# Gathering attention scores with one DMA per head, rows 13 partitions apart

## The chip, the cores and the metric

The kernel runs on one core of one Trainium2 chip. The metric is the device time of one execution in microseconds; a profiled execution also leaves a trace, from which the rows below are read. The engines are named as in the profile: PE (matmuls; PEld is its weight loads), DVE, ACT, POOL and SP, whose queue issues nearly all DMAs here.

## The reference

Attention with a mix over heads before and after the softmax, followed by a gated expert layer. Batch 4, 12 heads, 448 positions, head dimension 64; the layer has 1,792 tokens, width 768 and inner width 1,536. All in float32.

```python
def _attn_ref(q, k, v, w_pre, w_post):
    scores = (1 / sqrt(64)) * matmul(q, k.transpose(0, 1, 3, 2))
    scores = einsum('bhij,hg->bgij', scores, w_pre)       # pre-mix over heads
    scores = scores - max(scores, axis=-1, keepdims=True)
    attn = exp(scores)
    attn = attn / (sum(attn, axis=-1, keepdims=True) + 1e-09)
    attn = einsum('bhij,hg->bgij', attn, w_post)          # post-mix over heads
    return matmul(attn, v)

def _moe_ref(x, w_gate, w_val, w_out, rms_g):
    xn = x / sqrt(mean(x * x, axis=-1, keepdims=True) + 1e-06) * rms_g
    g = xn @ w_gate
    return (g * (1 / (1 + exp(-g))) * (xn @ w_val)) @ w_out
```

## The kernel before, in words

**Chunks, slots, pairs.** Each of the four batches is cut into four chunks of query rows, 16 chunks in all (`n`). A chunk of 120 rows has 24 slots of `RH` = 5 query rows each: 12 slots in each half `u` of the 128 partitions. Two slots of a half are one pair step `p`; the chunks have 6, 6, 6 and 5 pairs (`PAIRS`), so there are 92 steps. The last chunk of a batch has ten slots in its first half and eight in the second.

**Scores, gather, pre-mix.** `qk_mm` computes the scores of two heads into two PSUM tiles, query rows on the partitions and 448 keys along them. `qk_evac` copies each to a staging tile `st` in SBUF (eight buffers; ACT takes the even head, DVE the odd one). The pre-mix needs, for one slot, the five rows of all 12 heads side by side on the partitions. That regrouping is a DMA from SBUF to SBUF, the *gather*: for each head and each half, SP issues one DMA that writes five partitions of the target `r`, 12 apart, with up to 12 slots in each, 448 float32 (1,792 bytes) a slot.

```python
for u in range(2):
    slots = 2 * (np_ - (u == 1 and halves_of(n, np_ - 1) == 1))
    rows = slice(64 * u + h, 64 * u + h + H * (RH - 1) + 1, H)
    nc.sync.dma_start(rt[n][rows, :slots], st[64 * u : 64 * u + RH * slots])
```

A chunk thus has 24 gathers. `r` is a rotating tile with two buffers, a new one for each chunk, so chunk `n` is gathered while chunk `n - 1` is consumed. `premix` multiplies the 60 rows of a half (`HR` = 12 x 5) with `wk_pre`, in which the pre-mix weights are spread over a mask, slot by slot.

**The order of the work.** The schedule is written out by hand, in program order for each engine. In step `t`, PE does the pre-mix of step `t`, the post-mix of step `t - 1`, a share of the attention-times-value products (`av_mm`) of an earlier chunk, and a share of the scores of the next chunk. DVE takes the row maxima, ACT the exponentials with their sums, POOL scales the post-mix weights. The scores of chunk `n` are spread over the steps of chunk `n - 1`, ending two steps before the chunk starts; their copies and gathers follow one step later. Loads (`q`, `k`, `v`), the stores of the attention output to DRAM (`xd`), its reading back as `sq` for the norm, and an early conversion of part of the expert weights (`wraw`, `wac`) are jobs at fixed steps. All of them go through SP's queue, in order. Before step 0 stands a prologue: loads, all scores of chunk 0, its gathers, the first pre-mix.

**After the steps.** The expert layer follows: products with weights and tokens split into two parts, three matmuls for each. From the third token tile on, its tiles take the two buffers of `r` over (`x_tile`).

`layout` prepares the inputs on the host: it orders the query rows of a chunk so that a half's rows stand as row-in-slot times slots, starting at partition 0 and 64, and it repeats the pre-mix weights and the mask to fit the rows of `r`.

Of the kernel before, what the change touches and what calls it, by code (L numbers as in the profile page):

```python
# [7 lines left out]
F32 = mybir.dt.float32  # L8
F32R = mybir.dt.float32r
# [7 lines left out]
B, H, S, D = 4, 12, 448, 64  # L17
DM, DFF = 768, 1536
RH = 5
CHUNK = 120  # L20
NC = 4
PAIRS = [6, 6, 6, 5]
OFF = [0, 120, 240, 360]
SP_ = 460
HR = H * RH
JT = 64
JC, JP = 4, 112
KT, FT = DM // 128, DFF // 128
# [5 lines left out]
def attention_moe(ctx: ExitStack, tc, q, k, v, wpre, wpost, mask, ident, wgv, wo, rms_g, out):  # L34
    nc = tc.nc
    NCHUNK = B * NC

    def pool(stack, name, bufs=1, **kw):
        return stack.enter_context(tc.tile_pool(name=name, bufs=bufs, reuse_waits="tile", **kw))
# [17 lines left out]
    pr = pool(ctx, "pr", 2)  # L57
# [10 lines left out]
    wk_pre = cst.tile([128, 64], F32, name="wk_pre")  # L68
    wk = cst.tile([128, HR], F32, name="wk")

# [4 lines left out]
    def load_consts():  # L75
        nc.sync.dma_start(msk.rearrange("p a r -> p (a r)"), mask)
        nc.sync.dma_start(we, wpre)
        nc.sync.dma_start(wp, wpost)

    def setup():  # L80
        nc.vector.tensor_scalar(we, we, D ** -0.5, None, ALU.mult)
        nc.vector.memset(wk_pre, 0.0)
        for i, (o, w) in enumerate(((wk_pre[:, :HR], we), (wk, wp))):
            m = msk[:, i].unsqueeze(1).to_broadcast([128, H, RH])
# [3 lines left out]
    kt, qt, vt, rt, sps, et, sm, wn, at, pm, nmx, qps, xps, xt = ({} for _ in range(14))  # L88
# [18 lines left out]
    def halves_of(n, p):  # L107
        return 1 if n % NC == NC - 1 and p == PAIRS[-1] - 1 else 2

    def qk_mm(n, hp):  # L110
        ps = [ps_q.tile([128, 512], F32, name="qk", tag="qk") for _ in range(2)]
        for u in range(2):
            for j in range(2):
                sl, m = slice(64 * j, 64 * j + 64), slice(64 * u, 64 * u + 64)
                nc.tensor.matmul(ps[j][m, :S], qt[n][sl, hp, m], kt[n // NC, hp][sl], start=True, stop=True)  # L115
        qps[n, hp] = ps

    def qk_evac(n, hp, j):
        h, np_ = 2 * hp + j, PAIRS[n % NC]
        ps = qps[n, hp][j]  # L120
        st = pq.tile([128, S], F32, name="st", tag="st", bufs=8)
        if j:
            nc.vector.tensor_copy(st, ps[:, :S])  # L123
        else:
            nc.scalar.activation(st, ps[:, :S], AF.Copy)  # L125
        if h == 0:
            rt[n] = pr.tile([128, 2 * KT, S], F32, name=f"r{n}", tag="r")
        for u in range(2):
            slots = 2 * (np_ - (u == 1 and halves_of(n, np_ - 1) == 1))
            rows = slice(64 * u + h, 64 * u + h + H * (RH - 1) + 1, H)  # L130
            nc.sync.dma_start(rt[n][rows, :slots], st[64 * u : 64 * u + RH * slots])

    def premix(n, p):
        ps = [ps_s.tile([128, 512], F32, name="sp", tag="sp") for _ in range(halves_of(n, p))]
        for v_ in range(2):
            for u in range(len(ps)):
                sl = slice(64 * u, 64 * u + HR)
                o = ps[u][64 * v_ : 64 * v_ + 64, :S]
                nc.tensor.matmul(o, wk_pre[sl], rt[n][sl, 2 * p + v_], start=True, stop=True)  # L139
        sps[n, p] = ps  # L140
# [14 lines left out]
    def norm(n, p):  # L155
# [5 lines left out]
        nc.vector.reciprocal(r, t)  # L161
        wn[n, p] = pe.tile([128, 2, HR], F32, name="wn", tag="wn")
        for u in range(k_):
            nc.gpsimd.tensor_scalar(wn[n, p][:, u], wk, r[:, u : u + 1], 1.0, ALU.mult, ALU.mult)  # L164

    def postmix(n, p):
        ps = [ps_m.tile([128, 512], F32, name="pm", tag="pm") for _ in range(2)]
        e, w = et.pop((n, p)), wn.pop((n, p))
        for u in range(2):
            u_ = min(u, len(e) - 1)  # L170
            for c in range(JC):
                for m in range(2):
                    j = min(2 * c + m, S // JT - 1) * JT
                    for v_ in range(2):
                        sl = slice(64 * v_, 64 * v_ + HR)
                        at_ = (u * JC + c) * HR
                        o = ps[v_][64 * m : 64 * m + JT, at_ : at_ + HR]
                        nc.tensor.matmul(o, e[u_][sl, j : j + JT], w[sl, u_], start=True, stop=True)  # L178
        pm[n, p] = ps
# [15 lines left out]
    def av_mm(n, hp):  # L195
# [5 lines left out]
        for c_ in range(JC):  # L201
            for m in range(2 if c_ < JC - 1 else 1):
                sl = slice(64 * m, 64 * m + JT)
                for j in range(2):
# [98 lines left out]
    for n in range(NCHUNK):  # L303
        lo, hi = first[n + 1] + 1, first[n + 2] + 1
        for hp in range(H // 2):
            t = lo + hp * (hi - lo) // (H // 2)
# [7 lines left out]
    for n in range(NCHUNK):  # L314
        b, c = divmod(n, NC)
# [18 lines left out]
    def part_a(extra):  # L334
        for j in range(H // 4):
            load_q(0, j)
            load_k(0, j)
        load_consts()
        nc.vector.memset(ones, 1.0)
        for hp in range(H // 2):  # L340
            qk_mm(0, hp)
            for j in range(2):
                qk_evac(0, hp, j)
            if hp == 5:
                setup()
        load_q(1)
        nc.sync.dma_start(g_sb, rms_g)
        nc.sync.dma_start(eye, ident)
        done = []
        for t in range(T + 24):  # L350
            def back(lag):
                return steps[t - lag] if 0 <= t - lag < T else None

            if t == first[NCHUNK - 1]:
                qk_ctx.close()
                start_b()
            for f, *a in jobs_at[t]:
                f(*a)
            for a in done:
                x_store(*a)  # L360
            done = [(n, hp // 3) for n, hp in (av_at[t - 1] if t else []) if hp % 3 == 2]
            if back(0):
                premix(*back(0))
            for a in qk_at[t - 1] if t else []:
                for j in range(2):
                    qk_evac(*a, j)
            for a in done:
                av_copy(*a)
                av_sum(*a)
            if back(1):  # L370
                postmix(*back(1))
            for a in av_at[t]:
                av_mm(*a)
            for a in qk_at[t]:
                qk_mm(*a)
            if back(0):
                rowmax(*back(0))
                expo(*back(0))
            if back(1):
                for v_ in range(2):  # L380
                    evac_a(*back(1), v_)
            if back(0):
                norm(*back(0))
            extra(t - T)
            if t >= T + 6 and not done and not any(av_at[t:]):
                break
# [46 lines left out]
    def x_tile(i):  # L433
        if i < 2:
            t = b_pools["x"].tile([128, 2 * KT, S], F32R, name=f"x{i}", tag=f"x{i}")
        else:
            t = pr.tile([128, 2 * KT, S], F32R, name=f"x{i}", tag="r")
        return t[:, :KT], t[:, KT:]

    raws = {}  # L440
# [55 lines left out]
    w, xs, wos, hs, hr = {}, {}, {}, {}, []  # L496
# [219 lines left out]
def layout(inputs):  # L716

    import numpy as np

    q, k, v = inputs["q"], inputs["k"], inputs["v"]  # L720
    def pairs(x):
        return x.reshape(B, H // 2, 2, S, D).transpose(0, 2, 4, 1, 3).reshape(B, 2 * D, H // 2, S)

    qt = np.zeros((B, 2 * D, H // 2, SP_), np.float32)
    qt[..., :S] = pairs(q)
    ql = np.zeros((B, 2 * D, NC, H // 2, 2, 64), np.float32)
    for c, p in enumerate(PAIRS):
        for u in range(2):
            ns = 2 * (p - (u == 1 and c == NC - 1))
            r, s = np.meshgrid(np.arange(RH), np.arange(ns), indexing="ij")  # L730
            i = OFF[c] + u * 2 * RH * p + s * RH + r
            ql[:, :, c, :, u, : RH * ns] = qt[..., i.reshape(-1)]
    kl = pairs(k)
    vl = np.zeros((B, H, JC * 128, D), np.float32)
    vl[:, :, :S] = v
    vl = vl.reshape(B, H, JC, 128, D).transpose(0, 3, 1, 2, 4)

    def cols(w, kt):
        w = np.ascontiguousarray(w)
        if w.dtype != np.float64:  # L740
            raise TypeError(w.dtype)
        w = w.view(np.int64)
        return w.reshape(kt, 128, -1, 128).transpose(2, 1, 0, 3).reshape(-1, 128, kt, 128)

    def halves(x):
        return np.tile(np.pad(x, ((0, 64 - HR), (0, 0))), (2, 1))

    eye_r = np.eye(RH, dtype=np.float32)
    return {
        "q": ql.reshape(B, 2 * D, NC, H // 2, 128),  # L750
        "k": kl,
        "v": vl,
        "wpre": halves(np.tile(inputs["w_pre"], (RH, 1))),
        "wpost": halves(np.repeat(inputs["w_post"], RH, axis=0)),
        "mask": halves(np.concatenate([np.repeat(eye_r, H, axis=0), np.tile(eye_r, (H, 1))], axis=1)),
        "ident": np.eye(JP, dtype=np.float32),
        "wgv": np.concatenate([cols(inputs["moe_w_gate"], KT), cols(inputs["moe_w_val"], KT)], axis=2),
        "wo": cols(inputs["moe_w_out"], FT),
        "rms_g": inputs["moe_rms_g"].reshape(KT, 128).T,
    }  # L760
# [18 lines left out]
```

## Time and profile before

| | us |
|---|---|
| median of 3 runs (1039.56 to 1043.53) | 1042.5 |
| the profiled execution, own time | 1044.07 |
| its span | 1042.3 |
| PE busy in the span | 924.9 |
| DVE busy | 573.1 |
| ACT busy | 351.5 |
| POOL busy | 279.8 |

The mean granted clock of PE is 0.957 of full speed. Busy times overlap; PE's share of 89% is a mean over a stage that is nearly always busy and one that is not. Of the chain of work that ended last, PE holds 53%, DMA 19% (the gather `r<-st` alone 10%) and DVE 12%.

### The profile page before, as it was taken

Reading aid. Unit: us, or ns where it says so; the run is one execution under the profiler, and the core shown is the slowest. Engines: PE = TensorE matmul, PEld = TensorE weight load, DVE = VectorE, ACT = ScalarE, POOL = GpSimd, SP = SyncE. Lnnn points to the kernel's source line nnn. Section 1 sums busy time; section 2 is a strip of 40 time slices with the busy share of each in tenths; the row PEclk is TensorE's granted clock in tenths of the full one; section 3 lists DMA queues with packets and bytes.
Section 4 is the critical chain, followed back from the end, with each engine's and each line's share of the span. In section 5 each row is a group of like instructions: output and inputs, shape, how many; then the busy total and the mean of one; then the engine's idle time right before and its main releaser. Section 6 shows DMA issues by size and latency. Waiting matters only on the chain.

```text
span 1042.3 us, 29796 instructions
## 1 busy us (share of the span) xinstructions
PE 924.9 (89%) x12696; PEld 749.2 (72%) x12696; DVE 573.1 (55%) x990; ACT 351.5 (34%) x798; POOL 279.8 (27%) x349
## 2 busy tenths in 40 slices
PE   4669978887688688798989999999999999999998
PEld 0346655565356556565779999999999987999997
DVE  1447745764475466464495454555699977611100
ACT  1346635554554455566311101111111122421200
POOL 0011101111311221333445344444455562100000
PEclk9989989998898899898989999999999999999999
DMA  4535456545545545544422222122433346523100
GB/s 140 163 129 169 131 160 178 167 135 168 162 147 161 151 147 165 152 125 137 151 65 96 97 96 84 50 77 97 146 120 125 108 131 208 196 98 98 53 27 36
DMA packets 73108, 131.49 MB, mean 126 GB/s; under 512 B 19376, under 2 KB 63120, under 8 KB 72976
## 3 DMA queue, kind: packets, MB, share of 16 engines
q1 hardware_dynamic: 72688, 128.01, 38.5%
q8 instruction: 100, 1.64, 0.7%
q0 software_dynamic: 288, 1.57, 0.4%
q14 instruction: 32, 0.26, 0.1%
HBM read 67.90 MB, written 22.95 MB: 87 GB/s over the span
## 4 chain that ended last, share of the span: by engine, by line
PE 53%; DMA 19%; DVE 12%; ACT 5%; issue 4%; POOL 1%; SPq 1%; DVEq 0%; ACTq 0%; POOLq 0%
DMA r<-st 10%; PE po L493 6%; PE po L494 6%; PE po L492 6%; PE sp L139 4%; PE qk L115 4%; PE pm L178 4%; PE av L206 4%; PE pv L494 4%; PE pv L492 3%; PE pv L493 3%; DMA wraw<-in_wgv 3%; PE pg L492 3%; PE pg L494 3%; PE pg L493 3%
## 5 line engine op out<-in xcount | busy, mean ns | idle before, releaser
L152 ACT ACTIVATE e<-sp,nm 128x448 f32<-128x448 f32 x180 | 112.4, 629 | 166.0 <-DVE nm L145 166.0
L139 PE MATMUL sp<-r,wk_pre 60*64 60x448 f32 x720 | 124.3, 586 | 45.8 <-DMA r<-st 31.7
L178 PEld LDWEIGHTS pm<-wn,e 60*64 60x64 f32 x5888 | 115.8, 140 | 57.4 <-POOL wn L164 42.3
L164 POOL TENSOR_SCALAR wn<-wk,rp 128x60 f32<-128x60 f32 x180 | 55.1, 320 | 365.8 <-DVE rp L161 267.4
L115 PE MATMUL qk<-k,q 64*64 64x448 f32 x768 | 119.0, 602 | 23.6 <-ACT st L125 14.0
L145 DVE TENSOR_REDUCE nm<-sp 128x1 f32<-128x448 f32 x180 | 103.6, 616 | 55.5 <-PE sp L139 53.6
L206 PE MATMUL av<-a,v 64*64 64x120 f32 (+1 forms) x2688 | 107.1, 274 | 26.9 <-ACT xt L221 18.7
L178 PE MATMUL pm<-wn,e 60*64 60x60 f32 x5888 | 122.6, 226 | 6.4 <-issue 2.9
L139 PEld LDWEIGHTS sp<-r,wk_pre 60*64 60x64 f32 x720 | 45.1, 141 | 95.1 <-issue 47.5
L206 PEld LDWEIGHTS av<-a,v 64*64 64x64 f32 x2688 | 87.1, 141 | 32.4 <-ACT xt L221 19.8
L492 PE MATMUL pv<-x,wh 128*128 128x448 f32 x264 | 97.8, 371 | 2.3 <-ACT wh L424 2.3
L494 PE MATMUL pv<-x,wl 128*128 128x448 f32 x264 | 97.9, 371 | 1.2 <-POOL wl L425 1.2
L493 PE MATMUL pv<-x,wh 128*128 128x448 f32 x264 | 97.7, 370 | 0.0
L492 PE MATMUL pg<-x,wh 128*128 128x448 f32 x264 | 97.0, 367 | 0.0
L494 PE MATMUL pg<-x,wl 128*128 128x448 f32 x264 | 96.7, 366 | 0.0
L493 PE MATMUL pg<-x,wh 128*128 128x448 f32 x264 | 96.6, 366 | 0.0
L424 ACT ACTIVATE wh<-wc 128x768 fp32r<-128x768 f32 x26 | 22.0, 846 | 193.0 <-DVE wc L400 193.0
L523 POOL TENSOR_TENSOR g<-g,u 128x448 f32<-128x448 f32 x48 | 62.0, 1291 | 78.3 <-DVE u L522 53.2
L123 DVE COPY st<-qk 128x448 f32<-128x448 f32 x96 | 59.7, 622 | 41.0 <-PE qk L115 35.5
L425 POOL TENSOR_TENSOR wl<-wc,wh 128x768 fp32r<-128x768 f32 x26 | 48.7, 1873 | 110.9 <-ACT wh L424 110.9
L476 DVE TENSOR_TENSOR x<-hraw,x 128x448 fp32r<-128x448 f32 x48 | 33.1, 730 | 76.2 <-ACT x L475 76.1
L191 DVE COPY a<-pm 128x480 f32<-128x480 f32 x92 | 60.0, 652 | 12.0 <-PE pm L178 11.8
(120 smaller groups left out, 1640.4 us busy)
## 6 DMA issues: line engine op xcount, KB each, us to landing
r<-st SPq DMA_DIRECT2D x288, 105.0 KB
wraw<-in_wgv SPq DMA_DIRECT2D x20, 768.0 KB
hd<-sg SPq DMA_DIRECT2D x48, 224.0 KB
hraw<-hd SPq DMA_DIRECT2D x48, 224.0 KB
wraw<-in_wo SPq DMA_DIRECT2D x12, 768.0 KB
v<-in_v SPq DMA_DIRECT2D x12, 512.0 KB
q<-in_q SPq DMA_DIRECT2D x15, 384.0 KB
k<-in_k SPq DMA_DIRECT2D x12, 448.0 KB
```

The source lines that it names most:

```text
L115: nc.tensor.matmul(ps[j][m, :S], qt[n][sl, hp, m], kt[n // NC, hp][sl], start=True, stop=True)
L123: nc.vector.tensor_copy(st, ps[:, :S])
L139: nc.tensor.matmul(o, wk_pre[sl], rt[n][sl, 2 * p + v_], start=True, stop=True)
L145: nc.vector.tensor_reduce(t, ps[:, :S], AX.X, ALU.max, negate=True)
L152: nc.scalar.activation(e, ps[:, :S], AF.Exp, bias=nmx.pop((n, p, u)), accum_out=sm[n, p][:, u : u + 1])
L178: nc.tensor.matmul(o, e[u_][sl, j : j + JT], w[sl, u_], start=True, stop=True)
L191: nc.vector.tensor_copy(dst, src)
L206: nc.tensor.matmul(o[m][64 * j : 64 * j + 64].rearrange("p (u i) -> p u i", u=2), vt[b, h // 4][sl, h % 4, c_], at[n][sl, :, c_, h, :w], s ...
L492: nc.tensor.matmul(ps, a, xh[:, kk], start=(i == 0), stop=False)
L493: nc.tensor.matmul(ps, a, xl_[:, kk], start=False, stop=False)
L494: nc.tensor.matmul(ps, a2, xh[:, kk], start=False, stop=(i == n - 1))
L523: nc.gpsimd.tensor_tensor(g, g, u, ALU.mult)
```

## The change

The rows of a slot now stand 13 partitions apart (`GAP` = 13) and not 12: head `h`, row `r` of the first half at partition `h + 13 r`. Five steps of 13 are 65, so going on with the same stride puts row `r` of the second half at `64 + (h + 1) + 13 r`. One DMA with ten target partitions so writes both halves of a head. For the last head the second half would begin one row too far; it goes to row 64 in a DMA of its own, so that this head keeps two gathers. In the second half the heads stand rotated by one, and the weights and the mask are laid out to match. A chunk has 13 gathers in place of 24. The second half of `st` begins right behind the first and not at partition 64.

Between the blocks of twelve lie rows that no gather writes. The pre-mix now runs over 64 rows of a half, with zero weights in these, so what stands there must be finite. Therefore the two targets are no longer allocated anew for each chunk: they are two tiles that live through the attention steps, cleared once at the start, one by DVE and one by POOL. The expert layer's tiles take their place under the tags `r0` and `r1`. In the last chunk of a batch the second half is gathered with two slots that nobody reads.

```diff
+GAP = H + 1
...
+    r_two = [pr.tile([128, 2 * KT, S], F32, name=f"r{i}", tag=f"r{i}", bufs=1) for i in range(2)]
+    for n in range(NCHUNK):
+        rt[n] = r_two[n % 2]
...
-        if h == 0:
-            rt[n] = pr.tile([128, 2 * KT, S], F32, name=f"r{n}", tag="r")
-        for u in range(2):
-            slots = 2 * (np_ - (u == 1 and halves_of(n, np_ - 1) == 1))
-            rows = slice(64 * u + h, 64 * u + h + H * (RH - 1) + 1, H)
-            nc.sync.dma_start(rt[n][rows, :slots], st[64 * u : 64 * u + RH * slots])
+        w = 2 * RH * np_
+        if h < H - 1:
+            nc.sync.dma_start(rt[n][h : h + (2 * RH - 1) * GAP + 1 : GAP, : 2 * np_], st[: 2 * w])
+        else:
+            for u, at_ in enumerate((h, 64)):
+                nc.sync.dma_start(rt[n][at_ : at_ + (RH - 1) * GAP + 1 : GAP, : 2 * np_], st[u * w : u * w + w])
...
-                sl = slice(64 * u, 64 * u + HR)
+                sl = slice(64 * u, 64 * u + 64)
...
         load_consts()
+        nc.vector.memset(r_two[0], 0.0)
+        nc.gpsimd.memset(r_two[1], 0.0)
         nc.vector.memset(ones, 1.0)
...
-            t = pr.tile([128, 2 * KT, S], F32R, name=f"x{i}", tag="r")
+            t = pr.tile([128, 2 * KT, S], F32R, name=f"x{i}", tag=f"r{i % 2}", bufs=1)
...
+    mix = np.zeros((2, 64, H), np.float32)
+    row = np.zeros((2, 64, RH), np.float32)
+    for u in range(2):
+        for r in range(RH):
+            at = GAP * r + (np.arange(H) + u) % H
+            mix[u, at], row[u, at] = inputs["w_pre"], eye_r[r]
```

The order of the query columns in `layout` changes with the place of the second half.

## Rows read from the trace of the kernel before

**Rows 1.** Stretches: length, busy us of PE PEld DVE ACT POOL, clock, DMA share, GB/s.
```profile
7.70:28.00 20.30, 9.29 (x40) 1.95 (x40) 3.68 (x10) 2.72 (x5) 0.00 (x0) 1.00 0.30 104
32.44:474.50 442.06, 362.94 (x9784) 248.16 (x9784) 264.00 (x630) 235.69 (x599) 79.43 (x202) 0.92 0.49 152
474.50:1042.30 567.80, 550.92 (x2865) 498.75 (x2864) 304.66 (x350) 111.30 (x194) 200.12 (x144) 0.98 0.32 105
88.08:113.71 25.63, 22.50 (x656) 17.48 (x657) 17.26 (x38) 14.95 (x39) 3.40 (x12) 1.00 0.57 168
373.74:399.46 25.72, 21.67 (x649) 14.45 (x649) 18.98 (x51) 14.71 (x38) 3.59 (x12) 1.00 0.54 164
113.70:128.50 14.80, 14.78 (x464) 10.68 (x461) 11.60 (x26) 9.80 (x25) 2.39 (x8) 1.00 0.44 135
```

**Rows 2.** DMA issues by line, whole span: count, size of one.
```profile
r<-st SPq DMA_DIRECT2D x288, 105.0 KB
...
r<-st SPq DMA_DIRECT2D x48, 87.5 KB
...
r<-st SPq DMA_DIRECT2D x48, 70.0 KB
```

**Rows 3.** PE's waits, 32.4 to 474.5 us: total, times, longest (us).
```profile
PE sp L139 <- DMA r<-st: 31.7, 7, 8.6
PE av L206 <- ACT xt L221: 16.9, 4, 7.9
...
PE qk L115 <- ACT st L125: 11.4, 8, 4.1
...
PE av L206 <- DVE xt L224: 3.2, 3, 2.7
...
PE qk L115 <- DVE st L123: 2.2, 1, 2.2
```

**Rows 4.** The chain that ended last: start, length, what.
```profile
47.46 7.06 DMA r<-st
...
254.39 8.25 DMA sq<-xd
...
269.12 7.33 DMA sq<-xd
...
483.48 3.85 DMA xr<-xd
```

**Rows 5.** Granted clock of PE in 40 slices of the span, tenths.
```profile
PEclk9989989998898899898989999999999999999999
```

**Rows 6.** Instructions in order of time, 0 to 40 us: start, length, engine, line.
```profile
0.84 0.17 DVE L339 MEMSET ones<- 128x128 f32 x1 [0.84 <-PEq L768]
...
7.14 0.62 DVE L123 COPY st<-qk 128x448 f32<-128x448 f32 x1 [6.14 <-PE qk L115]
7.67 20.66 SPq L131 DMA_DIRECT2D r<-st  x24
...
19.80 0.62 DVE L123 COPY st<-qk 128x448 f32<-128x448 f32 x1 [1.90 <-PE qk L115]
...
20.46 0.11 DVE L82 MEMSET wk_pre<- 128x64 f32 x1
...
33.69 0.30 PEld L139 LDWEIGHTS sp<-r,wk_pre 60*64 60x64 f32 x6 [0.99 <-DMA r<-st]
...
38.00 0.59 POOL L164 TENSOR_SCALAR wn<-wk,rp 128x60 f32<-128x60 f32 x2 [37.55 <-DVE rp L161]
```

**Rows 7.** The gather's line: its issue on SP, ns min/median/max.
```profile
L131 SPq DMA_DIRECT2D r<-st x384: 732/733/1315, 7.7 to 452.5; - x192
```

**Rows 8.** The page's costliest groups: busy us, mean ns of one, idle before.
```profile
L139 PE MATMUL sp<-r,wk_pre 60*64 60x448 f32 x720 | 124.3, 586 | 45.8 <-DMA r<-st 31.7
...
L115 PE MATMUL qk<-k,q 64*64 64x448 f32 x768 | 119.0, 602 | 23.6 <-ACT st L125 14.0
```

**Rows 9.** SP's own waits, whole span: total, times, longest (us).
```profile
SPq L131 <- PE sp L139: 8.4, 4, 4.0
```

More of the change, by code (lines that the diff above doesn't have):

```diff
@@ L725, in layout @@
     qt[..., :S] = pairs(q)
-    ql = np.zeros((B, 2 * D, NC, H // 2, 2, 64), np.float32)
+    ql = np.zeros((B, 2 * D, NC, H // 2, 128), np.float32)
     for c, p in enumerate(PAIRS):
[L728 to L732, printed above, removed]
+        u, r, t = np.meshgrid(np.arange(2), np.arange(RH), np.arange(2 * p), indexing="ij")
+        i = np.minimum(OFF[c] + (u * 2 * p + t) * RH + r, SP_ - 1)
+        ql[:, :, c, :, : 4 * RH * p] = qt[..., i.reshape(-1)]
     kl = pairs(k)
@@ L748, in layout @@
     eye_r = np.eye(RH, dtype=np.float32)
+    mix = np.zeros((2, 64, H), np.float32)
[4 more added lines that the diff above has]
+            mix[u, at], row[u, at] = inputs["w_pre"], eye_r[r]
     return {
-        "q": ql.reshape(B, 2 * D, NC, H // 2, 128),
+        "q": ql,
         "k": kl,
         "v": vl,
-        "wpre": halves(np.tile(inputs["w_pre"], (RH, 1))),
+        "wpre": mix.reshape(128, H),
         "wpost": halves(np.repeat(inputs["w_post"], RH, axis=0)),
-        "mask": halves(np.concatenate([np.repeat(eye_r, H, axis=0), np.tile(eye_r, (H, 1))], axis=1)),
+        "mask": np.concatenate([row.reshape(128, RH), halves(np.tile(eye_r, (H, 1)))], axis=1),
         "ident": np.eye(JP, dtype=np.float32),
```

## Prediction

> **What bounds the kernel now.** I first split the span. Up to 32.44 us lies a prologue, from there to 474.5 us the attention steps, and after that the expert layer [rows 1]. Behind 474.5 us the matmul engine (PE) is busy for 550.92 of 567.8 us and no gather is issued, so I leave that stretch alone. In the attention steps PE is busy for 362.94 of 442.06 us at a granted clock of 0.92, a mean over its two levels (2.4 and 1.2 GHz). These 442 us, and the prologue, are what the change can reach.
>
> Next I asked what the gather (the copy of a head's scores from `st` into `r`) costs the DMA engines. In 7.7 to 28.0 us almost nothing but gathers is in flight, issued back to back; the DMA share is 0.30 at 104 GB/s [rows 1]. The share is a mean over 16 engines, so 0.30 x 16 = 4.8 engines are busy: a gather with five target partitions keeps five engines busy and leaves eleven idle. One busy engine moves 104 / 4.8 = 21.7 GB/s, or 1,792 bytes (one score row of 448 float32) in 83 ns.
>
> With that price I filled the attention steps. They hold the gathers of 15 chunks: 264 of 105.0 KB, 48 of 87.5 KB, 48 of 70.0 KB [rows 2], that is 36.1 MB (a KB is 1,024 bytes). At 21.7 GB/s this is 1,665 us of one engine, 333 us on each of five. All traffic of the stretch is 0.49 x 16 x 442 = 3,466 engine-us, so the rest is 1,801, or 113 us on each of sixteen. The five gather engines carry 333 + 113 = 446 us of work in 442 us. They are full, while the mean share of 0.49 looks harmless. **That is the bound of the stage.**
>
> The waits agree. PE sat idle for 31.7 us in seven waits for `r` at the head of a chunk, and for 16.9 + 11.4 + 3.2 + 2.2 = 33.7 us because ACT or DVE were late with `xt` and `st` [rows 3]. These engines are themselves held by transfers: the chain shows gathers taking 7.06 us and loads of `sq` taking 8.25 and 7.33 us, whereas a load issued after the last gather takes 3.85 us [rows 4]. A load that spreads over sixteen engines also has a share on the five full ones, and it lands when that share does. The clock row dips to 0.8 in several slices of this stage, and to no less than 0.9 after it [rows 5].
>
> **The change, part by part.**
>
> *One gather with ten target rows in place of two with five.* A six-pair chunk has 24 gathers of 60 packets, 12 packets on each of five engines: 288 per engine. After the change eleven gathers have 120 packets, and if they spread over ten engines that is again 12 per engine; the last head still needs two gathers with five rows, 2 x 12 more on five engines. So the fullest engines get 11 x 12 + 24 = 156 packets a chunk. A five-pair chunk goes from 12 x (10 + 8) = 216 to 11 x 10 + 20 = 130, its second half carrying two unused slots. Over the 15 chunks 4,032 becomes 2,236, or 0.555. The gather load on the fullest engines falls to 333 x 0.555 = 185 us, and with the rest to 298 us. That no longer fills the stage.
>
> That ten rows take ten engines is not in the trace of before; it has only five rows on 4.8 engines, and this is the row that I extend. The Trainium skill (DMA: Bandwidth & Descriptors, "Why a DMA increments its semaphore by 16 and not by 1") says that a hardware-generated copy uses the largest number of engines up to 16 that divides the slowest dimension on both sides. By that rule five target rows get five engines, with which the trace agrees (4.8), and ten rows against 120 or 100 source rows get ten; the sum by the rule is the same 298 us.
>
> *What is late next.* PE. Two six-pair chunks ran at clock 1.00 with PE busy for 22.50 and 21.67 us, and four steps of a five-pair chunk took 14.80 us with PE busy for 14.78, so 18.5 us for five [rows 1]. Twelve chunks at 22.1 and four at 18.5 make 339 us: a stage that is always fed. The rows also show that nothing else holds a fed step, since PE is then busy for 99% of it. To this I add what stays idle:
>
> - waits for `r` at a chunk's head: 3 of 31.7 us. The last gather of a chunk is due two steps after its scores are copied, some 7 us, and an undisturbed transfer took 3.85.
> - late `xt` and `st`: 10 of 33.7 us. The transfers behind them get shorter by about 7.5 - 3.85 = 3.6 us each; the longest waits keep a rest.
> - all other idle time, 442.06 - 362.94 - 31.7 - 33.7 = 13.7 us, kept whole.
> - a slower clock: PE work takes 362.94 us now against 339 at full clock, so dips cost 24 us; they follow idle stretches, and with 27 of 79 us of idle time left I keep 7.
>
> 339 + 3 + 10 + 13.7 + 7 = 373 us in place of 442: **69 us less**. Both ends: nothing but the 13.7 us stays, 353 us and 89 less; or half of every stall stays, 339 + 16 + 17 + 13.7 + 12 = 398 us and 44 less.
>
> *The prologue.* Scores of the last two heads are copied at 19.80 to 20.42 us, but 24 gathers leave SP only by 28.3 us and the second half of the first pre-mix starts at 33.69 [rows 6]. One gather costs SP 0.73 us [rows 7]. A pair of heads comes every 2.5 us; it now needs two issues (1.6 us with gaps) and 24 packets per engine (2.0 us), so neither SP nor the engines fall behind. The three last gathers leave by 20.4 + 3 x 0.81 = 22.8 us. Landing takes between 2.0 us (24 packets) and 3.85; at 3 us the pre-mix starts at 25.8. I take **7.5 us less**, between 6 and 9.
>
> *Issue on SP.* 384 issues become 176 + 32 = 208, so 176 x 0.73 = 128 us less of a queue that also issues the loads, over the whole stage. Bounds per issue are 0.73 and twice that for twice the rows; even twice, 176 x 1.46 + 32 x 0.73 = 280 us equals today's 281. It is not on the path; cost nothing, and a load gets out earlier behind a gather.
>
> *The two clears.* 12 x 448 = 5,376 elements a partition. The DVE rows of 128 and 64 elements take 0.17 and 0.11 us, so 0.94 ns an element and 5.1 us. DVE starts at 0.84 and is free at 6.1 with `ones`; its first score copy is at 7.14 [rows 6]. The loads and the first scores, for which it waits until then, cover it. Had an element twice the price, copies and gathers would start 4 us later and half the gain of the prologue were gone. The other clear is on POOL, whose first instruction of weight is at 38.00 us [rows 6] and whose target is not written before the second chunk's scores; nothing shows its price, but only above some 20 us (3.7 ns an element) would it matter. Nothing for both; at most 4 us lost.
>
> *Pre-mix over 64 rows in place of 60.* The 60-row pre-mix takes 586 ns, the 64-row score matmul of equal width 602 [rows 8]; at worst 16 ns x 720 = 12 us. The second mean holds other clocks and other waits, and the columns streamed are the same 448; I take nothing.
>
> *Kept targets.* A gather must still wait until the pre-mixes two chunks back have read the tile; that wait is here now (8.4 us in four) [rows 9] and stays. Behind it on SP stand the chunk's loads, as before.
>
> **Sum.** 1,042.3 - 69 - 7.5 = 965.8 us of span. The profiled execution took 1,044.07, 1.6 above the median 1,042.5; against the median the change gives 966.
>
> **Rivals.**
>
> *A: the gather gets no wider (0.10).* Then 120 packets fall on the same five engines, 24 each, and the load stays 446 us. Only issue time goes, which the prologue hides behind the full engines: 1,038 to 1,044. For it: no row shows ten. Against: 4.8 engines for five rows is too near five for chance. The Trainium skill (same page, "Rules for kernel authors") says that splitting a transfer into two partition halves doesn't help, as both spread over all sixteen engines. By that rule merging them would bring little, as in this rival; the share of 0.30 disagrees with it here, which is why it has a tenth.
>
> *B: ten engines, but slower packets (0.15).* In 88.08 to 113.71 us the share is 0.57 at 168 GB/s, 18.4 GB/s for a busy engine, 1.18 times dearer than alone (small packets of other transfers are in it) [rows 1]. If ten writers at once made a packet 1.5 times dearer, the fullest engines would carry 185 x 1.5 + 113 = 391 us and the stage about 400: 42 + 6 less, 994; 985 to 1,005.
>
> *C: slower (0.05).* The tile is now one object for the whole run, so a gather could be made to wait for an earlier gather into it. PE needs 22 us a chunk, so 13 gathers held for over 1.7 us each would again set the pace; over 442/15/13 = 2.3 us the stage is slower than now. At 3.85 us each, a chunk takes 50 us and the stage 750: about 1,350. Against: interleaved rows of one tile are gathered today 0.86 us apart [rows 6], far less than a landing.
>
> **How the numbers follow.** My forecast has 0.70: 966, by its bounds 944 to 992. The range reaches to the middle of B on the one side and, on the other, to a stage in which a third of the kept 13.7 us goes too: 938 to 1,000. Below it lies nearly nothing, above it A, C and part of B, 0.2 together. A time within 0.5% (5 us) of before is about what a measurement can't tell from no change; A gives 0.08 of that and 0.02 just beyond it on the fast side. Faster 0.70 + 0.15 + 0.02 = 0.87, same 0.08, slower 0.05.
>
> **What would show it.** Right: in the prologue a DMA share near 0.5 while gathers are in flight, SP free within 1 us of the last copy, and the first pre-mix near 26 us; in the steps almost no PE wait for `r`, PE busy near 350 of 373 us at a clock of 0.96 or more, loads of `sq` in 4 to 5 us. Wrong: a share that stays at 0.30 (A), chains of gathers still over 6 us at a higher share (B), gathers issued singly, one landing apart (C), or `xt` and `st` as late as today although gathers are quick, which would leave the stage near 398 us.

## The result and the profile after

The changed kernel takes 978.9 us (median of 4 runs, 977.7 to 982.5) against 1,043.0 for the kernel before in the same comparison: a ratio of 0.939, interval 0.936 to 0.943. That is 64 us less; 76.5 were forecast. The profiled execution has a span of 977.2 us. Two executions below, one of 978.0 us with the loads of `sq` early and one of 992.6 us with the small DMAs on POOL, took over 1.5% longer than the fastest of their kernel and are left out of its time and ratio.

First the same stretches as in [rows 1], cut where the same work begins and ends: gathers of the prologue, attention steps, expert layer (length, busy us of PE, PEld, DVE, ACT, POOL, granted clock, DMA share, GB/s).

```profile
7.64:22.80 15.16, 9.28 (x40) 1.94 (x40) 3.72 (x10) 2.72 (x5) 0.00 (x0) 1.00 0.51 156
26.10:409.60 383.50, 343.15 (x9784) 237.84 (x9784) 264.71 (x630) 235.23 (x599) 79.79 (x202) 0.98 0.61 177
409.60:977.20 567.60, 550.09 (x2865) 499.18 (x2864) 304.82 (x350) 111.50 (x194) 200.02 (x144) 0.98 0.32 105
```

The expert layer is unchanged (567.6 us against 567.8). The steps went from 442.06 to 383.50, 58.6 us less; the first pre-mix from 32.44 to 26.10, 6.3 us less. During the prologue's gathers the DMA share is 0.51 and no longer 0.30: 8.2 engines are busy on average where 4.8 were.

The prologue in order of time shows why it is shorter, and where the clears lie (start, length, engine, line).

```profile
0.74 4.58 POOL L345 MEMSET r<- 128x5376 f32 x1 [0.29 <-POOLq L779]
...
1.93 4.54 DVE L344 MEMSET r<- 128x5376 f32 x1 [1.93 <-issue]
...
6.45 0.17 DVE L346 MEMSET ones<- 128x128 f32 x1
...
7.11 0.62 DVE L128 COPY st<-qk 128x448 f32<-128x448 f32 x1 [0.50 <-PE qk L120]
7.64 13.46 SPq L133 DMA_DIRECT2D r<-st  x11
...
21.20 1.55 SPq L136 DMA_DIRECT2D r<-st  x2
...
27.04 0.30 PEld L144 LDWEIGHTS sp<-r,wk_pre 64*64 64x64 f32 x6 [0.69 <-DMA r<-st]
```

SP has issued its last gather at 22.75 us, not at 28.3 [rows 6]. DVE is free of its clears half a microsecond before its first score copy.

PE's waits in the steps, to be read beside [rows 3] (total, times, longest, us):

```profile
PE av L211 <- ACT xt L226: 12.8, 3, 6.0
PE av L211 <- issue: 6.8, 8, 1.9
PE pm L183 <- issue: 5.0, 9, 1.0
PE qk L120 <- ACT st L130: 4.4, 5, 1.3
...
PE sp L144 <- issue: 1.7, 2, 1.5
PE av L211 <- DVE xt L229: 1.7, 3, 1.2
PE qk L120 <- issue: 1.6, 3, 1.0
...
PE qk L120 <- DVE st L128: 0.8, 1, 0.8
```

The 31.7 us of waits for `r` at the head of a chunk are gone. Late `xt` and `st` fell from 33.7 to 12.8 + 4.4 + 1.7 + 0.8 = 19.7 us. Idle time of PE for which the profile shows no cause ("issue") rose.

The chain says what `xt` now waits for (start, length, what), beside [rows 4]:

```profile
135.86 4.81 DMA r<-st
...
175.84 4.39 DMA r<-st
...
220.41 2.60 DMA sq<-xd
...
225.09 5.67 DMA sq<-xd
...
291.76 7.25 DMA sq<-xd
```

Two gathers are left among the long pieces of the chain, of 4.39 and 4.81 us; before there were sixteen, most of them of 6.5 to 7.6. The chain's share of DMA fell from 19% to 7% of the span. Of the loads of `sq` some are still slow, 2.60 to 7.25 us. The clock row, beside [rows 5], has two slices at 0.8 in the steps, where before there were seven. Two more of before lie across the end of the steps and from 521 us on, and one of after, from 782 us on, lies in the expert layer; the prediction, which saw no dip below 0.9 behind the steps, overlooked the one from 521 us:

```profile
PEclk9999999998998999999999999999999989999999
```

### The profile page after: what moved, and what is told of

Read it like the earlier page. It is cut to its first block, busy times and chain, and to the rows that moved or that the text cites. A ratio compares the mean times of both kernels' runs of the same rounds, so it can differ in the third digit from the quotient of the medians.

```text
span 977.2 us, 29612 instructions
## 1 busy us (share of the span) xinstructions
PE 904.3 (93%) x12696; PEld 739.3 (76%) x12696; DVE 578.5 (59%) x991; ACT 351.3 (36%) x798; POOL 284.6 (29%) x350
## 4 chain that ended last, share of the span: by engine, by line
PE 65%; DVE 12%; DMA 7%; issue 5%; ACT 5%; POOL 2%; SPq 1%; DVEq 0%; ACTq 0%; POOLq 0%
PE pm L183 7%; PE sp L144 6%; PE po L500 6%; PE po L501 6%; PE po L499 6%; PE qk L120 6%; PE av L211 6%; PE pv L501 4%; PE pv L499 4%; PE pv L500 4%; PE pg L499 4%; PE pg L501 4%; PE pg L500 4%; DMA sq<-xd 3%; DMA wraw<-in_wgv 2%
## 5 line engine op out<-in xcount | busy, mean ns | idle before, releaser
L183 PEld LDWEIGHTS pm<-wn,e 60*64 60x64 f32 x5888 | 109.0, 135 | 57.9 <-POOL wn L169 41.7
L120 PE MATMUL qk<-k,q 64*64 64x448 f32 x768 | 115.5, 584 | 15.6 <-ACT st L130 7.0
L211 PE MATMUL av<-a,v 64*64 64x120 f32 (+1 forms) x2688 | 102.8, 267 | 25.0 <-ACT xt L226 15.0
L183 PE MATMUL pm<-wn,e 60*64 60x60 f32 x5888 | 117.2, 221 | 8.5 <-issue 5.0
L144 PE MATMUL sp<-r,wk_pre 64*64 64x448 f32 x720 | 114.1, 558 | 9.1 <-DMA g_sb<-in_rms_g 6.4
L150 DVE TENSOR_REDUCE nm<-sp 128x1 f32<-128x448 f32 x180 | 103.8, 617 | 19.1 <-PE sp L144 16.4
L211 PEld LDWEIGHTS av<-a,v 64*64 64x64 f32 x2688 | 82.7, 136 | 30.5 <-ACT xt L226 16.2
L144 PEld LDWEIGHTS sp<-r,wk_pre 64*64 64x64 f32 x720 | 43.0, 135 | 52.3 <-ACT e L157 20.4
L196 DVE COPY a<-pm 128x480 f32<-128x480 f32 x92 | 60.0, 653 | 11.6 <-PE pm L183 11.2
```

What stands on the lines that cost most here:

```text
L150: nc.vector.tensor_reduce(t, ps[:, :S], AX.X, ALU.max, negate=True)
L196: nc.vector.tensor_copy(dst, src)
L211: nc.tensor.matmul(o[m][64 * j : 64 * j + 64].rearrange("p (u i) -> p u i", u=2), vt[b, h // 4][sl, h % 4, c_], at[n][sl, :, c_, h, :w], s ...
```

## The experiments

Each run was compared with the kernel before on its own chip; ratios are to that. Theory W is the prediction's: five full DMA engines set the pace, and wider gathers free them. The rivals put the gain down to the layout (L) or to fewer issues and transfers (I).

**Five target rows again, all else as changed.**

```diff
-        if h < H - 1:
-            nc.sync.dma_start(rt[n][h : h + (2 * RH - 1) * GAP + 1 : GAP, : 2 * np_], st[: 2 * w])
-        else:
-            for u, at_ in enumerate((h, 64)):
-                nc.sync.dma_start(rt[n][at_ : at_ + (RH - 1) * GAP + 1 : GAP, : 2 * np_], st[u * w : u * w + w])
+        for u, at_ in enumerate((h, 64 + (h + 1) % H)):
+            nc.sync.dma_start(rt[n][at_ : at_ + (RH - 1) * GAP + 1 : GAP, : 2 * np_], st[u * w : u * w + w])
```

> The new layout, the kept targets, their clears and the 64-row pre-mix stay; each head is gathered by two DMAs with five target rows again, 24 a chunk. Theory W (the width of a gather made the gain): the fullest engines carry 288 packets a chunk again, the prologue's share is near 0.30, the first pre-mix starts at about 33 us, and the time is 1,040 to 1,052 us (the second half of each last chunk carries two slots more than before, 96 packets in 4,032, so up to 8 us above before). Rival L (the layout and the kept targets made it): about 979.

Measured: 1,046.7 us, ratio 1.003 (0.999 to 1.006). The stretches of its trace, prologue and steps:

```profile
7.70:28.00 20.30, 8.94 (x40) 1.64 (x32) 3.62 (x9) 2.72 (x5) 0.00 (x0) 1.00 0.31 109
32.00:477.00 445.00, 370.62 (x9784) 248.96 (x9784) 264.48 (x630) 235.31 (x599) 79.51 (x202) 0.92 0.50 153
```

The share is back at 0.31, the steps at 445 us, the clock at 0.92. The layout, the kept targets and the 64 rows bring nothing; L is out. This run undoes width and issue count together.

**The width kept, the issues put back.**

```diff
             nc.sync.dma_start(rt[n][h : h + (2 * RH - 1) * GAP + 1 : GAP, : 2 * np_], st[: 2 * w])
+            nc.sync.dma_start(tiny[:1, H * n + h : H * n + h + 1], ones[:1, :1])
```

> The changed kernel, and behind each of the first eleven gathers of a chunk one more DMA of 4 bytes on SP into a scratch tile, so that a chunk issues 24 DMAs as before, at the new width. Theory W: SP's queue has room, 975 to 985 us. Rival I (fewer issues on SP and fewer transfers in flight made the gain): most of it goes, 1,015 to 1,045 us.

Measured: 998.4 us, ratio 0.957 (0.952 to 0.961), between the two ranges. Width alone is worth 1.003 - 0.957, some 48 us; the smaller number of issues 0.957 - 0.939, some 18 us (a 4-byte DMA stands in for a gather here). SP's queue in the prologue shows part of that price:

```profile
14.87 0.59 SPq L135 DMA_DIRECT2D tiny<-ones  x1
15.56 0.82 SPq L134 DMA_DIRECT2D r<-st  x1
16.43 0.59 SPq L135 DMA_DIRECT2D tiny<-ones  x1
17.12 0.82 SPq L134 DMA_DIRECT2D r<-st  x1
...
24.93 1.61 SPq L138 DMA_DIRECT2D r<-st  x2
```

A gather every 1.56 us, 3.1 us for a pair of heads that comes every 2.5: SP sets the pace, and the first pre-mix starts at 29.21 us, 3.1 later than after the change. The steps are 17.0 us longer than after it:

```profile
29.21:429.70 400.49, 348.77 (x9784) 240.80 (x9784) 263.89 (x630) 235.53 (x599) 79.63 (x202) 0.97 0.58 170
```

PE's waits for `r`, gone after the change, are back in them: 8.9 us in four. PE's busy time is 5.6 us longer, at a clock of 0.97.

**The small DMAs on POOL's queue.** The same edit with `nc.gpsimd.dma_start`.

> The eleven extra 4-byte DMAs a chunk, which cost 19 us when SP issued them, are issued by POOL. Theory Q (SP's queue was the price: 605 ns for each, and what stands behind it): the loss goes, 977 to 983 us. Rival: the number of transfers in flight or on the engines was the price: it stays at 992 to 1,002.

Measured: 986.8 us, ratio 0.944 (0.937 to 0.950), runs from 976.4 to 988.7. That lies between the two ranges, nearer to theory Q's, and an issue costs POOL 0.52 us too. The run of 976.4 us is the one with a trace. In it SP issues the first eleven gathers in 13.46 us, as after the change, the first pre-mix starts at 27.43 us, PE waits for no `r` in the steps, and they take 382.47 us. So in that run the price of the steps is gone with the issues on SP; why the other runs are 10 to 12 us longer stays open.

**Half the bytes, in three forms.** Gathers that copy 224 of 448 keys: ten rows and 13 issues a chunk; five rows and 12 issues; five rows and 24 issues. The edit of the first:

```diff
-: 2 * np_], st[: 2 * w])
+: 2 * np_, : S // 2], st[: 2 * w, : S // 2])
```

> The gathers copy only the first 224 of 448 keys (the rest of r stays zero, so the scores of half the keys are left out); packets as many, half as long. It asks what is left of the gather's price in the changed kernel. If the loads of sq and wraw are still late because gathers stand before them (rival G), the idle time of PE for late xt and st (19.7 us) falls by more than half and the time to 955 to 967 us. If those loads are late by their own chain of buffers (theory S), it stays within 6 us: 973 to 979.

> Half the keys again as in the run before with 224 keys, one DMA a head as there, but with five target rows of 24 slots in place of ten rows of 12 (a slot's first half in one part of the tile, its second behind it; the second half of the pre-mix reads zeros, so the output is left wrong in these parts). As many packets and bytes as in that run and one issue a chunk fewer; only the number of engines differs. Theory W (what counts is the load of the fullest engine): 288 packets of 896 bytes on five engines are about as much as 156 of 1,792 bytes, so the time is near that of the changed kernel, 970 to 985 us, and the prologue's share near 0.25. Rival I (issues count, not engines): it stays with the run of half the keys, 952 to 962.

> The run with two five-row gathers a head (24 issues a chunk), copying 224 of 448 keys, so the scores of half the keys are left out. Width and issues are those of the kernel before, only the bytes are halved. If the full engines were what bound it (theory W), the load of the fullest falls to 288 packets of 896 bytes a chunk, some 14 us beside 22 of PE, and the time to 970 to 990 us: that of the five-row run with 12 issues (961) and up to 19 us for the issues. If 24 transfers a chunk, each landing singly, were the bound whatever they carry (rival I), it stays above 1,015.

The second form writes five rows of 24 half slots:

```diff
+        halved = rt[n].rearrange("p s (a j) -> p (s a) j", a=2)
+        nc.sync.dma_start(halved[h : h + (RH - 1) * GAP + 1 : GAP, : 4 * np_], st[: 2 * w, : S // 2])
```

Measured, beside the full-size runs (us and ratio):

| target rows | issues a chunk | 448 keys | 224 keys |
|---|---|---|---|
| 5 | 24 | 1,046.7 (1.003) | 988.8 (0.947) |
| 10 | 24 (11 of them of 4 bytes) | 998.4 (0.957) | - |
| 10 | 13 | 978.9 (0.939) | 957.9 (0.918) |
| 5 | 12 | - | 961.0 (0.921) |

The kernel with five rows and 24 issues gets 58 us faster when only its bytes are halved: W for the kernel before holds. But at half the bytes the width is worth nothing that can be told (intervals 0.913 to 0.923 and 0.918 to 0.924), and my expectation for the second form, 970 to 985, was wrong. By the prediction's price its fullest engines carry 333 / 2 + 113 = 280 us in steps of some 367. Half a row costs more than half in its trace, though: in 7.7 to 20 us the prologue moves 82 GB/s at a share of 0.28, 18.3 GB/s for a busy engine, by which the load is some 315 us (an estimate). That is about the load after the change, as I had expected, and yet the time is some 18 us less. So a load of 280 to 315 us on the fullest engines costs nothing that can be told beside the ten-row form's 185 / 2 + 113 = 205, while 446 us in 442 set the pace. With 24 issues in place of 12, five rows and half the bytes cost 0.947 - 0.921, some 28 us more.

Half the bytes still save 21 us after the change. The first pre-mix starts 2.3 us earlier and the steps are 19.1 us shorter, 7.2 of it in PE's busy time:

```profile
23.81:388.20 364.39, 335.98 (x9784) 233.58 (x9784) 264.49 (x630) 234.70 (x599) 79.55 (x202) 0.99 0.49 137
```

PE's waits in that stretch:

```profile
PE av L211 <- ACT xt L226: 9.6, 4, 4.1
PE qk L120 <- ACT st L130: 4.8, 6, 1.1
PE pm L183 <- issue: 4.6, 10, 0.8
...
PE qk L120 <- issue: 1.4, 2, 1.1
...
PE av L211 <- DVE xt L229: 0.7, 3, 0.2
PE av L211 <- issue: 0.6, 2, 0.4
```

The time, 957.9 us, lies in the range of rival G (gathers stand before the loads), but its mechanism isn't what is seen: late `xt` and `st` fell from 19.7 to 15.1 us, not by half. More came from idle time marked "issue", 15.1 to 6.6 us, and from PE's busy time. The clock doesn't explain the latter: PE is busy for 335.98 us at 0.99 here and for 341.69 at 1.00 in the next run. Why fewer bytes shorten both stays open; the run also leaves half the scores zero, and nothing here parts that from the bytes.

**The loads of `sq` early.**

```diff
-    sq[b, kk] = pq.tile([128, S], F32, name="sq", tag="sq", bufs=2) if kk else sums[b]
+    sq[b, kk] = pq.tile([128, S], F32, name="sq", tag="sq", bufs=5) if kk else sums[b]
...
-            job(t + kk // 2, sq_load, b, kk)
+            job(t - 1 + kk // 2, sq_load, b, kk)
```

> The changed kernel with five buffers for sq in place of two and its loads issued one step earlier. Theory S (ACT waits for sq loads that wait on SP for POOL to free one of two buffers, and PE waits for ACT's xt): the three stretches with steps of 7 to 13 us shrink to ordinary steps, 12 to 20 us less, 959 to 967. Rival G (the loads are slow because gathers stand before them): under 5 us less, 974 to 979.

Measured: 966.2 us, ratio 0.926 (0.920 to 0.932), some 14 us less than the change alone (0.939 - 0.926) and, with the next run, the fastest full kernel here. Its steps:

```profile
25.88:398.20 372.32, 341.69 (x9784) 237.94 (x9784) 264.38 (x630) 234.65 (x599) 79.52 (x202) 1.00 0.63 183
```

372.3 us against 383.5, at a clock of 1.00 (its level of 2.4 GHz). In its list of PE's waits the 12.8 us for ACT's `xt` are gone; what leads it is idle time without a releaser:

```profile
PE pm L183 <- issue: 11.3, 11, 1.9
PE qk L120 <- ACT st L130: 4.3, 5, 1.4
PE qk L120 <- issue: 3.2, 4, 2.1
```

SP's queue shows the same chain. After the change SP stood before loads of `sq` until POOL had freed a buffer:

```profile
SPq L244 <- POOL sum L250: 16.8, 8, 5.6
```

That wait is gone too with five buffers, and so are ACT's waits for `sq` and `sum` (9.2 and 5.4 us). This bears theory S out: the loads were late by their own two buffers or their late issue (both are changed here and not told apart). The gain lies in the expected 12 to 20 us, though the interval reaches to some 7.

**The loads of `wraw` early too.** From the second group of weights on, the load of a group goes out at the fourth of the seven jobs of the group before it.

> The run with five sq buffers, and the loads of wraw also issued four steps earlier. DVE then no longer waits for wraw (7.3 us in four waits after the change). If that wait reaches PE, 3 to 7 us less than with sq alone, 961 to 966; if not, the same 965 to 970.

Measured: 967.9 us, ratio 0.929 (0.925 to 0.932), no difference from `sq` alone. DVE's wait for `wraw` is gone from the trace, so it didn't reach PE.

**The same for the kernel before.** The edit of the `sq` loads, made there.

> The kernel before with five sq buffers and the sq loads one step earlier, nothing else. After the change this took 10 us off. If the five full engines set the pace of the stage before (theory W), moving loads about gains nothing there: 1,038 to 1,045. If the stalls on sq were a cost of their own, it gains as much as after: 1,030 to 1,035.

Measured: 1,041.1 us, ratio 0.998 (0.995 to 1.001). What takes some 14 us off after the change takes nothing that can be told off before it. The trace, of the fastest of the ten runs (1,035.2 us), shows part of the wait moving: late `xt` falls from 20.1 to 5.1 us, and PE's waits for DMAs before pre-mixes rise from 31.9 to 39.3.

**Both clears on DVE.**

```diff
-        nc.gpsimd.memset(r_two[1], 0.0)
+        nc.vector.memset(r_two[1], 0.0)
```

> Both clears on DVE, one behind the other (4.54 us each), so that DVE is free at about 11.1 us and its first score copy comes 4 us late. The prediction priced such a delay at half the gain of the prologue: the first pre-mix 3 to 4 us later than 26.1, and 981 to 983 us. Rival: SP and the engines catch up before the last head, and the pre-mix starts within 1 us of 26.1: 978 to 980.

Measured: 986.7 us, ratio 0.948 (0.944 to 0.952). The cover is gone:

```profile
7.54 4.54 DVE L345 MEMSET r<- 128x5376 f32 x1 [1.07 <-issue]
...
12.14 0.56 DVE L128 COPY st<-qk 128x448 f32<-128x448 f32 x1
...
26.14 1.55 SPq L136 DMA_DIRECT2D r<-st  x2
...
32.02 2.56 PE L144 MATMUL sp<-r,wk_pre 64*64 64x448 f32 x8 [7.40 <-DMA eye<-in_ident]
```

The first copy is 5.0 us late, no part of it is caught up, and the first pre-mix is 5.9 us late. Nearly the whole gain of the prologue hung on the second clear being on POOL. The time is above the expected 981 to 983; by the ratios some 9 us are lost, 3 more than the prologue shows, which the intervals can hold.

**The pre-mix over 60 rows.**

```diff
-                sl = slice(64 * u, 64 * u + 64)
+                sl = slice(64 * u, 64 * u + HR)
```

> The changed kernel with the pre-mix over 60 rows of a half again (rows 60 to 63, the last query row of four heads, are left out). If the four more rows cost nothing, as the prediction took it, 976 to 982 us and the same mean of a pre-mix matmul at full clock within 5 ns. If they cost the 16 ns a matmul of its upper bound, 967 to 970.

Measured: 980.3 us, ratio 0.940 (0.936 to 0.944), no difference from the change. The four more rows cost nothing that can be told; the prediction's upper bound of 12 us would have been seen.

## Why the prediction was right, point by point

**The bound.** Right: the gather's engines were full. With five rows restored the stage is back at 445 us; with half the bytes in those, 58 us go; another stall removed brings nothing before.

**Ten rows on more engines.** Right: the share went from 0.30 to 0.51, 8.2 engines with gaps between the gathers, and rival A falls with it. The rule of the Trainium skill (DMA: Bandwidth & Descriptors, "Why a DMA increments its semaphore by 16 and not by 1"), which gives such a copy ten engines, fits; the ten itself stands in no row. The Trainium skill's rule on partition halves (same page, "Rules for kernel authors") speaks of halves that each spread over all sixteen engines, which these halves of five rows don't.

**What is late next.** PE, as said: fed PE with its remaining clock dips was put at 339 + 7 = 346 us and is 343.15, at a clock of 0.98. Waits for `r` were put at 3 us and are nothing. **The term that was mis-sized is late `xt` and `st`: 10 us forecast, 19.7 measured.** I had the transfers behind them get shorter by 3.6 us each, as if gathers alone made them late; the run with five `sq` buffers shows that 12.8 us of it was the loads' own chain. The last term, all other idle time, was kept at 13.7 us and is 383.50 - 343.15 - 19.7 = 20.6. The stage so came out at 383.5 for 373, within its bounds of 353 to 398.

**The prologue.** 6.3 us for 7.5. The issue went as worked out (22.75 for 22.8); landing took 3.4 us for the first half and 4.3 to the second, where I had taken 3. Part of the miss is in the sum: 25.8 lies 6.6 us before 32.44, where the first half of the pre-mix started, and 7.9 before the 33.69 of the second; the 7.5 mixed the two.

**Issue on SP.** Priced at nothing, since even doubled it would equal today's total. That step was wrong: with the width in place, 24 issues a chunk cost some 18 us. A sum over a queue doesn't show what stands behind it, and SP's pace in the prologue shows that a queue that is idle on average can be the slowest link in a burst. The total was not harmed, since the change removes both, and that is luck: the prediction put its 69 us in the steps down to width, while of the whole gain width alone, at the old number of issues, brings some 48. Some 15 of the 58.6 us in the steps came from the term that it had put at nothing.

**The clears.** Hidden, as said, but with 0.5 us to spare and not 1.0: DVE's began at 1.93 us, not 0.84, though it took 4.54 for 5.1. POOL's, unpriced, took 4.58. The price without cover was put at half the prologue's gain and is 5.9 of 6.3 us.

**Rival B.** In the prologue a busy engine moves 156 / (0.51 x 16) = 19.1 GB/s for 21.7, so a byte is 1.14 times dearer with ten rows: the direction of B, far from its 1.5. At that price the fullest engines carry 185 x 1.14 + 113 = 324 us after the change and not 298, still well under 383.5. **Rival C** did not occur: eleven gathers leave in 13.5 us.

**Two signs that were not met.** SP was to be free within 1 us of the last copy and was so 2.4 us after it (20.39 to 22.75); the prediction's own sum, 22.8, did not agree with this sign. Loads of `sq` were to take 4 to 5 us and take 2.60 to 7.25.

## What to carry to other kernels

A mean DMA share of a third or a half can hide full engines: divide it by the engines that a transfer's shape can use, and compare their load with the length of the stage. While engines are full, removing another stall can bring nothing, as with `sq` here; once they are freed it is next, so read the waits again. The price of an issue is not its sum over the stage; look at what a burst of them holds back.

## What was not expected of the hardware

Idle time of PE before an instruction that waited for nothing the profile shows grew as the stage got denser: in the steps the waits marked "issue" among those listed add up to 8.2 us before the change, 15.1 after it and 19.5 with `sq` early (11.3 of it before post-mix matmuls in eleven waits). With half the bytes it falls from the 15.1 to 6.6 us, but with five rows and 24 issues it rises, from 8.1 to 11.6, so the bytes alone don't set it. No run here tells what it is.
